# Keys with values in the second layer: five runs of small matmuls instead of eight

## The chip, the cores and the metric

The kernel runs on one core of a Trainium2 chip. The time is the device time of one execution, in microseconds (us), median of several runs. The engines are TensorE (PE: matmuls, and transposes as matmuls), VectorE (DVE), ScalarE (ACT), GpSimd (POOL) and SyncE (SP), which here issues the DMA transfers. Each engine works through its own queue of instructions in order, and waits on semaphores for what other engines must have finished.

## The reference

Four residual steps on x, 2048 rows of 640 columns: linear attention with learned features, a dense layer with mish, and the same two again with the same weights. What the change touches is the attention:

```python
qkv = (x @ wqkv).reshape(B, S, 3, H, Dh)            # H = 32 heads of Dh = 20
pk = jnp.einsum("bhsd,hdf->bhsf", k, w_phi)         # the same for q
phi_k = jnp.concatenate([softmax(pk), softmax(-pk)], axis=-1)
kv = jnp.einsum("bhsf,bhsd->bhfd", phi_k, v)
z = jnp.einsum("bhsf->bhf", phi_k)
o = einsum(phi_q, kv) / (einsum(phi_q, z) + 1e-6)
return o @ wo
```

`x` is layer-normalized ahead of it, and the result is added to x.

## The kernel before

**Tiles and stages.** The rows are cut into NB = 8 blocks of 256, a block into BT = 2 tiles of 128; tile i belongs to block i // 2. A layer's attention has two stages. The first (`attend_first`) goes through all blocks, projects them onto keys, queries and values, makes the features of keys and queries, and adds up features of keys times values over all rows in one PSUM tile, `kva`; the column of ones in each head's values makes z beside kv. The second (`attend_second`) turns `kva` into the weights `kvb` (L814), averages with them (L844), and projects with wo. The change concerns the first stage of the second layer (`layer` is 1); what comes ahead of it is the first layer's dense stage.

**A step.** A block has six steps, mostly in the order k0, k1, v0, v1, q0, q1 (keys, values and queries of its two tiles; the last block's q1 lies in stage 2, among its averages). Each step is a generator. `project` is 30 matmuls (L451): 5 slices of 128 columns, two halves, three products each, since a number is held as a high part (`xth`, weights `r1h`/`r2h`) and a low part (`xtl`, `r1l`/`r2l`). The low parts of the next block are made by POOL in three pieces, `lower` at L384: two of 128x512 for two slices each, and a third, 128x256, for the fifth slice. Within `project_half` the fifth slice's low part is first read by the 15th matmul.

**Features** (`features`, from L462). ACT evacuates the product (L135) into a `big` tile for keys, into `r210`/`r211` (the text of the profile has `r`) for queries; POOL has set their last columns to zero before (L467). DVE takes the largest and smallest of each head (L477), one engine subtracts the largest (L478: DVE for keys, POOL for queries), DVE the smallest (L480); ACT takes exp; DVE sums (L488) and inverts (L489); POOL multiplies by the inverse (L491, 128x1280). Queries are then transposed by DVE (L563, L561) and stored by SP in four transfers (L566) to `e_d`, from where stage 2 loads them (L783, L794, L796, L801) into `big` and `ol`.

**The sum.** When the features of keys are there, the generator `keys` goes on through some empty steps, `held(i)` of them, and then issues the tile's 32 matmuls of 40 columns into `kva` (L548; the profile counts 64 for a tile, 128 for two). `advance` moves all generators on by one step, the newest first, so `held` sets behind which step a tile's sum stands in PE's queue. In the second layer the two tiles of a block stand in one run behind the next block's first keys, the sum of block 1 behind block 2's second values, and the last block's at the end.

**Values** (`values`, `v_halves` at L142) are written by ACT into one tile of the pool `v` (2 buffers, one copy of 640 columns and one of the 32 ones), or into two smaller tiles of the pool `ol` (6 buffers, two copies of 320 and two of 16 ones), if `apart` is true. Features of keys lie in `big` (5 buffers).

**Order.** The order in which instructions enter the queues is that of a scheduler, which takes the program's order, its waits and `issue_after` into account. A shift on one engine therefore moves the order on others.

## Time and profile before

| what | value |
|---|---|
| median of three runs | 1348.87 us (1348.83 to 1349.65) |
| the profiled execution | 1349.24 us, of it the span 1347.4 |
| PE busy in 770 to 800 us | 30.00 of 30 us |
| DVE, ACT, POOL busy in 770 to 800 us | 25.69, 12.27, 17.16 us |
| granted clock of PE | 1.00 in all stretches looked at |

The times in all rows are microseconds from the start of the span. A row of the timeline has start, duration, engine, line, operation, output and inputs, shapes and a count; in brackets stands how long the engine was idle before, and what it waited for. Several instructions of one kind in a row are one line, with their common duration. A row of the chain of waits has start, duration, engine, line and count. The first stage of the second layer runs from about 694 us to 902 us.

### The profile page before, as it was taken

The numbers are of one execution on the slowest core, as the hardware profiler recorded it, in microseconds if no ns is written. First come the engines' busy times: TensorE is split into PE (matmuls) and PEld (weight loads), VectorE is DVE, ScalarE is ACT, GpSimd is POOL, SyncE is SP. The second block draws the span as 40 slices with busy tenths as digits, with TensorE's granted clock in tenths as the row PEclk, the third lists the DMA queues.
The fourth block names the chain that finished last, engine by engine and source line by source line (L and its number), as shares of the span: only waits on it lengthen the run. The fifth ranks groups of instructions, "written<-read, shape, count | busy, mean of one in ns | idle before, by whom it ended". The sixth has DMA issues, their size and how long they took to land.

```text
span 1347.4 us, 31386 instructions
## 1 busy us (share of the span) xinstructions
PE 1342.2 (100%) x13056; PEld 1333.4 (99%) x13056; DVE 1045.7 (78%) x1741; ACT 577.3 (43%) x986; POOL 480.2 (36%) x479
## 2 busy tenths in 40 slices
PE   9999999999999999999999999999999999999999
PEld 9999999999999999999999999999999999999998
DVE  6998898976787877778769788789759776676775
ACT  5444453223445545455443334332236444444443
POOL 3366554334322222222225556634352111111112
PEclk9999999999999999999999999999999999999999
DMA  9634446698703443234564534548873331233300
GB/s 329 195 91 91 95 87 148 167 268 304 221 18 87 118 118 81 56 100 114 152 213 111 130 80 96 94 111 265 262 270 107 79 91 23 84 98 99 79 21 21
DMA packets 353359, 174.24 MB, mean 129 GB/s; under 512 B 288193, under 2 KB 324785, under 8 KB 353217
## 3 DMA queue, kind: packets, MB, share of 16 engines
q1 hardware_dynamic: 353217, 172.25, 47.1%
q8 instruction: 102, 1.67, 0.5%
q14 instruction: 40, 0.33, 0.1%
HBM read 106.34 MB, written 65.86 MB: 128 GB/s over the span
## 4 chain that ended last, share of the span: by engine, by line
PE 100%; issue 0%; ACT 0%; DVE 0%; POOL 0%; POOLq 0%
PE mm L451 28%; PE one L969 25%; PE mm L1020 24%; PE one L451 13%; PE mm L844 3%; PE one L367 2%; PE one L548 2%; PE one L1020 1%; PE one L844 1%; PE one L92 0%; PE mm L274 0%; PE one L274 0%; PE mm L318 0%; ACT r1h L135 0%; PE one L811 0%
## 5 line engine op out<-in xcount | busy, mean ns | idle before, releaser
L995 POOL TENSOR_TENSOR ol<-big,ol 128x512 fp32r<-128x512 f32 (+1 forms) x98 | 131.9, 1346 | 471.7 <-ACT ol L994 411.6
L1020 PE MATMUL mm<-r2h,ol 128*128 128x320 f32 x1240 | 295.8, 309 | 0.0
L969 PE MATMUL one<-xtl,r1h 128*128 128x256 f32 x960 | 268.4, 280 | 0.0
L969 PE MATMUL one<-xth,r1l 128*128 128x256 f32 x960 | 268.2, 279 | 0.0
L969 PE MATMUL one<-xth,r1h 128*128 128x256 f32 x960 | 266.1, 280 | 0.0
L1020 PEld LDWEIGHTS mm<-r2h,ol 128*128 128x128 f32 x1240 | 212.1, 188 | 0.0
L1020 PE MATMUL mm<-r2l,ol 128*128 128x320 f32 x620 | 190.9, 309 | 0.0
L451 PE MATMUL mm<-r1h,xth 128*128 128x304 f32 (+1 forms) x600 | 184.6, 308 | 0.4 <-DVE r1l L334 0.4
L451 PE MATMUL mm<-r1l,xth 128*128 128x304 f32 (+1 forms) x600 | 183.7, 306 | 0.0
L451 PE MATMUL mm<-r1h,xtl 128*128 128x304 f32 (+1 forms) x600 | 183.5, 306 | 0.0
L969 PEld LDWEIGHTS one<-xth,r1l 128*128 128x128 f32 x960 | 180.5, 188 | 0.0
L969 PEld LDWEIGHTS one<-xtl,r1h 128*128 128x128 f32 x960 | 180.4, 188 | 0.0
L969 PEld LDWEIGHTS one<-xth,r1h 128*128 128x128 f32 x960 | 179.8, 188 | 0.0
L984 DVE TENSOR_SCALAR big<-big 128x512 f32<-128x512 f32 (+1 forms) x98 | 55.6, 567 | 120.8 <-ACT big L982 116.3
L982 ACT ACTIVATE big<-one,b1s 128x256 f32<-128x256 f32 x192 | 80.8, 468 | 102.4 <-PE one L969 102.1
L994 ACT ACTIVATE ol<-big 128x512 fp32r<-128x512 f32 (+1 forms) x98 | 60.8, 620 | 136.5 <-DVE big L993 136.4
L491 POOL TENSOR_TENSOR r<-r,r 128x1280 f32<-128x1280 f32 x32 | 79.0, 2468 | 110.6 <-DVE r L489 94.5
L1020 PEld LDWEIGHTS mm<-r2l,ol 128*128 128x128 f32 x620 | 116.5, 188 | 0.0
L986 ACT ACTIVATE big<-big,two 128x512 f32<-128x512 f32 (+1 forms) x98 | 70.1, 715 | 105.6 <-DVE big L985 105.5
L451 PEld LDWEIGHTS mm<-r1h,xth 128*128 128x128 f32 x600 | 112.8, 188 | 0.9 <-ACT r1h L135 0.5
L451 PEld LDWEIGHTS mm<-r1l,xth 128*128 128x128 f32 x600 | 112.8, 188 | 0.1
L451 PEld LDWEIGHTS mm<-r1h,xtl 128*128 128x128 f32 x600 | 112.8, 188 | 0.0
(179 smaller groups left out, 3132.9 us busy)
## 6 DMA issues: line engine op xcount, KB each, us to landing
e_d<-r SPq DMA_DIRECT2D x128, 160.0 KB, 4.0
big<-e_d SPq DMA_DIRECT2D x30, 640.0 KB, 8.9
x_d<-xt SPq DMA_DIRECT2D x23, 640.0 KB, 6.2
xt<-x_d SPq DMA_DIRECT2D x22, 640.0 KB, 5.3
n_d<-xn SPq DMA_DIRECT2D x168, 80.0 KB, 2.2
xt<-in_x SPq DMA_DIRECT2D x16, 640.0 KB, 4.6
xn<-x_d SPq DMA_DIRECT2D x28, 320.0 KB, 4.8
v<-n_d SPq DMA_DIRECT2D x30, 256.0 KB, 3.1
```

The costliest lines, as they stand in the source:

```text
L367: nc.tensor.transpose(ps[:, c, t * P:(t + 1) * P], self.rows[t][:, (c0 + c) * P:(c0 + c + 1) * P], ident)
L451: last_product[0] = nc.tensor.matmul(ps[:, :w], a[:, sl], r, start=(k == 0 and n == 0), stop=(k == KD - 1 and n == 2)).ins
L491: ins = scale.tensor_tensor(eg, eg, r.unsqueeze(2).to_broadcast([P, 2 * H, DH]), op=ALU.mult).ins
L548: nc.tensor.matmul(kva[32 * j:32 * j + DH + 1, 40 * r:40 * r + 40], v[1][c][:, (DH + 1) * g:(DH + 1) * (g + 1)], e[:, 40 * h:40 * h + 40], ...
L844: nc.tensor.matmul(po[c][64 * q:64 * q + 64, GW * j:GW * j + w], phs[g][:n, s0:s0 + 64], kvb[:n, g, :w], start=True, stop=True)
L969: nc.tensor.matmul(ph[:, j, :], l, r, start=(n == 0), stop=(n == 3 * KD - 1))
L982: exps[0] = nc.scalar.activation(part(ta, 0)[:, j - js.start], ph[:, j, :], AF.Exp, bias=b1s[:, 2 * pr + j:2 * pr + j + 1]).ins
L984: nc.vector.tensor_scalar_min(e, e, E_CAP)
L986: nc.scalar.activation(r, n, AF.Ln, bias=two)
L994: nc.scalar.activation(ah[:, js], n, AF.Copy)
L995: nc.gpsimd.tensor_tensor(al[:, js], n, ah[:, js].bitcast(F32), op=ALU.subtract)
L1020: ins = nc.tensor.matmul(pys[t][c][:, :HC], (ah, ah, al)[n][:, j, t * P:(t + 1) * P], w, start=(f == 0 and n == 0), stop=(f == KF - 1 and ...
```

## The change

`held` gets other numbers for the second layer, so that a sum of four tiles stands in one run: blocks 1 and 2 behind the first keys of block 3, blocks 3 and 4 behind the first keys of block 5, blocks 5 and 6 behind the first keys of block 7. Blocks 0 and 7 keep runs of two. As the values of two blocks then live at once, the second layer's blocks 4 and 6 put theirs in tiles of `ol`, as block 2 already did.

```diff
@@ -515,8 +515,8 @@
         def held(i):
 
             b, t = divmod(i, BT)
-            if layer and b == 1:
-                return 2
+            if layer and b in (1, 3, 5):
+                return 5 if b == 1 else 7 - t
             if not layer and b < 2:
                 return ((3, 1), (4, 1))[b][t]
             if not layer and b < NB - 2:
@@ -695,7 +695,7 @@
                 order = ("v0", "k0", "q0", "v1", "k1", "q1")
             elif b == NB - 1:
                 order = ("k0", "k1", "v0", "v1", "q0")
-            vs = [v_halves(b == 2 or (not layer and b % 2 == 0)) for _ in range(BT)]
+            vs = [v_halves(b % 2 == 0 and (b or not layer)) for _ in range(BT)]
             if 2 <= b < 2 + KD and not layer:
                 with tc.issue_after(last_act[0]):
                     o_ws.append(next(o_gen))
```

Three places in the queues, for the prediction. On PE, the sum of block 5 (`v` are its values, `r1h_...` the weights of the products around it, 64 matmuls a row) stood between the first and second keys of block 6:

```order
 L451 MATMUL mm<-r1l_8933,xth 128x304
 L451 MATMUL mm<-r1h_8932,xtl 128x304
-L548 MATMUL one<-big,v 21x40 x64
 L451 MATMUL mm<-r1h_8924,xth 128x304
 L451 MATMUL mm<-r1l_8925,xth 128x304
```

It is gone there; two blocks' sums now stand behind the first keys of block 7, those of block 6 (whose values are in `ol`) ahead of those of block 5:

```order
 L451 MATMUL mm<-r1l_8933,xth 128x304
 L451 MATMUL mm<-r1h_8932,xtl 128x304
+L548 MATMUL one<-big,ol 21x40 x64
 L548 MATMUL one<-big,v 21x40 x64
 L451 MATMUL mm<-r1h_8924,xth 128x304
```

The products themselves keep their order. On POOL, in block 3, where the low parts of block 4 are made (`xtl`, L384; `r_9941` and `r_9983` are the queries of block 2, `big` the keys of block 3), before:

```order
L491 TENSOR_TENSOR r_9941<-r_9941,r 128x1280
L384 TENSOR_TENSOR xtl<-xn,xth 128x512
L491 TENSOR_TENSOR r_9983<-r_9983,r 128x1280
L491 TENSOR_TENSOR big<-big,r 128x1280
L384 TENSOR_TENSOR xtl<-xn,xth 128x512
L467 MEMSET r_10281 128x32
L384 TENSOR_TENSOR xtl<-xn,xth 128x256
L491 TENSOR_TENSOR big<-big,r 128x1280
```

and now, where the queries of block 2 have other numbers:

```order
L491 TENSOR_TENSOR r_9877<-r_9877,r 128x1280
L491 TENSOR_TENSOR r_9919<-r_9919,r 128x1280
L384 TENSOR_TENSOR xtl<-xn,xth 128x512
L467 MEMSET r_10281 128x32
L491 TENSOR_TENSOR big<-big,r 128x1280
L384 TENSOR_TENSOR xtl<-xn,xth 128x512
L491 TENSOR_TENSOR big<-big,r 128x1280
L384 TENSOR_TENSOR xtl<-xn,xth 128x256
```

The first piece has moved behind the second query tile's L491, and the third behind the L491 of the second keys. On DVE, where stage 2 begins (`r_11637` is the first query tile of block 7, `kvb` the weights of the averages), before:

```order
L561 STREAM_TRANSPOSE r_11343<-r_11343 128x1280
L477 TENSOR_REDUCE m<-r_11637 128x32 x2
L814 TENSOR_TENSOR kvb<-one,mask 120x4x63 x2
L814 TENSOR_TENSOR kvb<-one,mask 120x3x63
L480 TENSOR_TENSOR r_11637<-m,r_11637 128x32x20
L853 TENSOR_SCALAR den<-mm 128x24
```

and now, the same tile under another number:

```order
L561 STREAM_TRANSPOSE r_11291<-r_11291 128x1280
L477 TENSOR_REDUCE m<-r_11649 128x32 x2
L480 TENSOR_TENSOR r_11649<-m,r_11649 128x32x20
L814 TENSOR_TENSOR kvb<-one,mask 120x4x63 x2
L814 TENSOR_TENSOR kvb<-one,mask 120x3x63
L853 TENSOR_SCALAR den<-mm 128x24
```

L480 has moved ahead of the three L814. In block 3, DVE's transposition of the first query tile (L563), too, stands earlier than before, ahead of the second keys' L477; and on SP the early loads of stage 2 into `ol` (L794, L796, L801) stand later.

## Prediction

> **What bounds the kernel now.** I read the page's busy shares first, then the list of TensorE's (PE's) waits, and then, for the stretch that the change touches, the chain of waits and the timelines of PE, POOL, DVE, ACT and SP.

> ```profile
> PE 1342.2 (100%) x13056; PEld 1333.4 (99%) x13056; DVE 1045.7 (78%) x1741; ACT 577.3 (43%) x986; POOL 480.2 (36%) x479
> ```

> ```profile
> PE one L92 <- POOL ident masks.py:199: 1.3, 1, 1.3
> PE mm L451 <- DVE r1l L334: 0.4, 1, 0.4
> PE one L274 <- issue: 0.2, 1, 0.2
> ```

> The whole span is matmul time: PE waits three times, 1.9 us in all, all at the start and none in the second layer. So the change can gain only what it takes out of PE's own stream, and it loses whatever wait it creates. The second layer's first stage in the chain of waits, one block of it, 27.2 us:

> ```profile
> 797.19 1.41 PE one L548 x126
> 798.60 25.78 PE mm L451 x180
> ```

> **What goes: three runs of small matmuls, not the matmuls.** A run of two tiles stands so on PE's timeline (start, duration of one or of the group):

> ```profile
> 796.75 0.30 PE L451 MATMUL mm<-r1l,xth 128*128 128x304 f32 x1
> 796.89 0.30 PE L451 MATMUL mm<-r1h,xtl 128*128 128x304 f32 x1
> 797.12 1.48 PE L548 MATMUL one<-big,v 128*21 128x40 f32 x128
> 798.52 0.41 PE L451 MATMUL mm<-r1h,xth 128*128 128x304 f32 x1
> 798.77 0.30 PE L451 MATMUL mm<-r1l,xth 128*128 128x304 f32 x1
> ```

> Projection matmuls start 0.14 us apart. From the last before the run (796.89) to the second behind it (798.77) it is 1.88, where two steps would take 0.28: the run costs 1.60. Its 128 matmuls span 1.48 less the last one's own duration, about 0.20 (an estimate: the profile gives the group only), so they are 10 ns apart, 1.28 together. The rest, 0.32 us, is paid once per run. The same number comes from the averages of stage 2, which already have a run of 88 and one of 176 matmuls:

> ```profile
> 902.13 0.30 PE L451 MATMUL one<-r2h,xtl 128*128 128x304 f32 x1
> ...
> 905.30 0.30 PE L451 MATMUL one<-r2l,xth 128*128 128x304 f32 x1
> ...
> 920.43 0.31 PE L451 MATMUL one<-r2h,xtl 128*128 128x320 f32 x1
> ...
> 926.18 0.31 PE L451 MATMUL one<-r2l,xth 128*128 128x320 f32 x1
> ```

> 88 take 3.17 - 0.28 = 2.89 and 176 take 5.75 - 0.29 = 5.46; two short runs less one long are 0.32. The 5-us run shows no slowing within. The change makes 8 runs into 5: **-0.95 us** (0.32 x 3), which I take as firm.

> **What is added on ACT.** Four value tiles are copied in halves.

> ```profile
> 751.42 0.77 ACT L135 ACTIVATE ol<-mm 128x320 f32<-128x320 f32 x2 [2.33 <-PE mm L451]
> 780.22 0.70 ACT L135 ACTIVATE v<-mm 128x640 f32<-128x640 f32 x1 [2.41 <-PE mm L451]
> ```

> Two halves take 0.07 us more than a whole, and a little again for the ones columns. ACT waits 2.3 to 2.4 us for PE ahead of these copies, and nothing on PE waits for them now: 0. Without that cover it would be 4 x 0.15 = 0.6.

> **What is moved on SP.** The `ol` tiles are held by values for longer, so stage 2's early loads into `ol` are issued later in SP's queue, and those queued behind them with them; the last wait for the run behind block 7's first keys, at about 879.

> ```profile
> 879.69 0.95 SPq L783 DMA_DIRECT2D big<-e_d x2
> 902.36 1.38 PE L844 MATMUL mm<-kvb,big 120*64 120x63 f32 x40
> ```

> ```profile
> big<-e_d SPq DMA_DIRECT2D x30, 640.0 KB, 8.9
> ```

> Before, the two loads of `big` stand at the same point, and their first reader, L844, starts 22 us later; from issue to landing such a load takes 8.9 us at the median. Six more in the same place share the queues, so I allow twice that, 18: 0, and up to 3 us if they took 25.

> **What is moved on POOL, third block.** The orders shown above put POOL's residual piece (L384) of the next block, first part, behind the second L491, and the third part behind one L491 on `big` more. Before:

> ```profile
> 782.68 1.29 POOL L384 TENSOR_TENSOR xtl<-xn,xth 128x512 fp32r<-128x512 f32 x1 [3.18 <-ACT xth L135]
> 785.26 2.37 POOL L491 TENSOR_TENSOR r<-r,r 128x1280 f32<-128x1280 f32 x1 [1.29 <-DVE r L489]
> 787.59 2.37 POOL L491 TENSOR_TENSOR big<-big,r 128x1280 f32<-128x1280 f32 x1
> 789.92 1.30 POOL L384 TENSOR_TENSOR xtl<-xn,xth 128x512 fp32r<-128x512 f32 x1
> 791.15 0.17 POOL L467 MEMSET r<- 128x32 f32 x1
> 791.23 0.75 POOL L384 TENSOR_TENSOR xtl<-xn,xth 128x256 fp32r<-128x256 f32 x1
> 791.93 2.38 POOL L491 TENSOR_TENSOR big<-big,r 128x1280 f32<-128x1280 f32 x1
> ```

> POOL works without a gap from 785.26. With the first L384 (1.3, until now in an idle stretch) and the second `big` (2.3) in that chain, the third part ends 3.6 later: 791.98 + 3.6 = 795.6. PE needs it in the 15th matmul of the next block's first keys. Those 30 matmuls end at the run at 797.1, so they start 30 x 0.14 earlier, at 792.8, and need it at 794.8; with one run switch gone already, 794.5. That is 1.1 late. DVE brings the second L491 its input earlier or later by some tenths, since it now transposes the first query tile ahead of the second keys, and both it and POOL follow a PE that is 0.3 ahead; by 0.8 earlier at best. Stall 0.3 to 1.1; I take **+0.7**, between.

> The lateness goes on into the fourth block, where the evacuation of its first queries (ACT `r<-mm`) must be done before PE can go on into the fifth block's keys:

> ```profile
> 789.56 0.68 ACT L135 ACTIVATE r<-mm 128x608 f32<-128x608 f32 x1 [2.55 <-DMA e_d<-r]
> 795.57 0.82 DVE L480 TENSOR_TENSOR r<-m,r 128x640 f32<-128x640 f32 x1 [2.67 <-POOL r L478]
> ```

> In the third block this copy ends at 790.2, 2.6 us ahead of the keys at 792.8. POOL and DVE enter the fourth up to 3.6 late less the 0.7 that PE itself stalls: 2.9 against 2.6. Bounds 0 (DVE's idle of 2.67 takes it up) and 0.5; **+0.2**. The blocks behind keep their order of residuals: 0.

> [...]

> ```profile
> 755.83 0.76 DVE L480 TENSOR_TENSOR big<-m,big 128x640 f32<-128x640 f32 x1
> 756.05 2.76 POOL L491 TENSOR_TENSOR r<-r,r 128x1280 f32<-128x1280 f32 x1 [0.81 <-DVE r L489]
> 778.30 1.88 DVE L478 TENSOR_TENSOR big<-big,m 128x640 f32<-128x640 f32 x1
> ```

> [...]

> **What is moved on DVE, start of stage 2.** L480 on block 7's first queries now stands ahead of the three L814, which make the weights of PE's first average.

> ```profile
> 899.84 1.50 DVE L477 TENSOR_REDUCE m<-r 128x32 f32<-128x640 f32 x2
> 901.63 1.01 DVE L814 TENSOR_TENSOR kvb<-one,mask 120x252 f32<-120x252 f32 x3 [0.29 <-PE one L811]
> 902.55 0.82 DVE L480 TENSOR_TENSOR r<-m,r 128x640 f32<-128x640 f32 x1
> ```

> ```profile
> 900.70 1.27 POOL L478 TENSOR_TENSOR r<-r,m 128x640 f32<-128x640 f32 x1 [1.86 <-DVE m L477]
> ```

> L480 waits for POOL's L478, which ends at 901.97; behind it stand L814, and behind L814 all of PE. So L480 runs to 902.8 and the first L814 (a third of 1.01) to 903.15. PE starts the average at 902.36 now, and so about as early with the terms above added up (-0.95 + 0.9): 0.8 late. DVE comes to L477 without a wait (its row names none), so it need not come forward when PE does; if it doesn't and PE has kept its 0.95, it is 1.75, and 2.2 with some tenths of lateness more. I take **+1.6**, nearer the upper end, since lateness adds.

> **Sum.** -0.95 + 0.7 + 0.2 + 1.6 = +1.55 us. The profiled execution took 1349.24 (span 1347.4), the median of the runs is 1348.87; on the median it makes **1350.4**.

> **Rivals.**
> 1. The stalls don't come: DVE and POOL find the idle time that their rows show (2.67 and 1.86 us of waits) and L480 is done in time. Then only the runs count, 1348.87 - 0.95 = **1347.9**. Against it: PE has no wait today, so nothing absorbs a late `kvb`.
> 2. Slower by more than 0.2%: DVE's two-operand steps fall under POOL's now gapless chain. Each such meeting costs DVE 1.06 (1.88 - 0.82), and a block that enters more than 2.6 us late passes it on. It decides if the fourth block ends later than it began: then the copies of queries are late for the sixth and seventh block too, by one meeting each: -0.95 + 0.7 + 0.2 + 2.1 + 2.2 = +4.25, **1353.1**. For it: the memsets and L491 stand in a new order in every block. Against it: in 80 us of blocks POOL has about 33 us idle and DVE 16:

> ```profile
> 800.00:880.00 80.00, 80.00 (x916) 79.34 (x914) 63.84 (x71) 30.62 (x45) 47.22 (x36) 1.00 0.42 80
> ```

> 3. The long runs slow down, since more weights are loaded in a row without a wide matmul to hide them: if the second half of each took half as long again, 0.64 a run, it is +1.9 on the sum, **1352.3**. Against it: the run of 176 above.
> 4. The loads are late for stage 2 by 3 us: -0.95 + 0.9 + 3 + 1.6, **1353.4**.
> That the runs don't merge at all is excluded by PE's order.

> **How the numbers follow.** The forecast has 0.50, rival 1 has 0.15, rival 2 0.23, rival 3 0.05, rival 4 0.04; 0.03 is left for a gain that I see no source for. 0.2% is 2.7 us, about what a measurement of this kernel can tell from no change. The forecast and rival 1 lie within it; rivals 2 and 4 outside, and half of 3. A tenth of the forecast (all its terms at their upper ends, +2.85) too. So faster 0.03, same 0.62, slower 0.35. Range: its low end is rival 1 with its own run-to-run spread, 1347.7; at the top it takes in rival 2 and a little of what may stall beyond it, to 1353.5. The likeliest case alone is 1349.1 to 1351.8.

> **What would show it.** Right: the chain has five L548 runs, three of about 2.9 us; PE's waits have new lines, L451 on POOL's `xtl` near 794 and L844 on DVE's `kvb` near 902, of some 0.7 and 1.6 us. Wrong: a wait of L451 on ACT or `r` in the fifth block or later over 0.5 us (rival 2), L844 on a DMA (rival 4), L548 of 256 longer than 3 us (rival 3), or no waits (rival 1). The sum itself is wrong if the three long runs save another amount than 0.3 each.

## Result and profile after

The change takes 1360.32 us (median of five runs, 1358.04 to 1361.01) against 1349.07 before (1348.83 to 1350.29): ratio 1.0078, interval 1.0067 to 1.0088, slower by 11.3 us. The prediction was 1350.4, within 1347.7 to 1353.5.

The page of the changed kernel, its row of busy times, and the list of PE's waits:

```profile
PE 1346.3 (99%) x13056; PEld 1338.0 (98%) x13056; DVE 1046.6 (77%) x1741; ACT 577.8 (43%) x994; POOL 481.3 (35%) x479
```

```profile
PE one L548 <- issue: 7.3, 3, 2.8
PE one L92 <- POOL ident masks.py:199: 1.3, 1, 1.3
PE mm L451 <- DVE r1l L334: 0.4, 1, 0.4
```

One line is new, and it is none of the waits that the prediction had named: PE stops three times in L548, 7.3 us in all, with no wait that the profile can name ("issue"). The list has no wait on `xtl`, `r` or `kvb`. The chain of waits shows where (start, duration, what):

```profile
768.14 2.12 PE one L548 x195
770.26 2.52 issue
772.78 0.76 PE one L548 x57
773.54 52.92 PE mm L451 x360
826.47 2.34 PE one L548 x217
828.81 1.98 issue
...
886.82 2.83 issue
```

Each long run is broken once. The products behind it take longer, too: 360 of them had 25.80 + 25.78 = 51.58 us before, now 52.92. The timeline of PE shows the break within the run, and the products behind it:

```profile
768.07 1.44 PE L548 MATMUL one<-big,ol 128*21 128x40 f32 x126
769.31 0.22 PE L548 MATMUL one<-big,v 128*21 128x40 f32 x2
769.33 0.21 PE L548 MATMUL one<-big,ol 128*21 128x40 f32 x2
769.35 0.90 PE L548 MATMUL one<-big,v 128*21 128x40 f32 x69
772.78 0.76 PE L548 MATMUL one<-big,v 128*21 128x40 f32 x57 [2.52 <-issue]
...
774.72 0.46 PE L451 MATMUL mm<-r1h,xth 128*128 128x304 f32 x1
774.98 0.46 PE L451 MATMUL mm<-r1l,xth 128*128 128x304 f32 x1
...
777.77 0.30 PE L451 MATMUL mm<-r1l,xth 128*128 128x304 f32 x1
777.91 0.30 PE L451 MATMUL mm<-r1h,xtl 128*128 128x304 f32 x1
```

Counted up, the stop comes behind the 199th matmul (126 + 2 + 2 + 69), in the midst of a tile whose first matmuls have been through: no matmul there has new data to wait for. In the second and third run it comes behind the 222nd and the 245th. Behind the stop the products are 0.25 us apart for three microseconds, and then 0.14 again. The table by stretches gives the granted clock there (it is the number ahead of the last two):

```profile
773.00:778.00 5.00, 5.00 (x76) 4.94 (x62) 3.02 (x4) 0.00 (x0) 1.99 (x2) 0.66 0.02 3
831.00:837.00 6.00, 6.00 (x63) 5.94 (x48) 2.26 (x3) 0.00 (x0) 2.52 (x2) 0.72 0.01 3
890.00:896.00 6.00, 6.00 (x32) 6.00 (x33) 2.74 (x4) 0.06 (x1) 2.37 (x1) 0.72 0.78 260
```

The lost clock is 0.34 x 5 + 0.28 x 6 + 0.28 x 6 = 5.1 us; within the first stretch, from 774.1 to 777.3, the clock is 0.50. A stop also costs more than its idle time: by PE's timeline, from the last product ahead of the first run (767.83) to the second behind it (773.72), less two steps, it is 5.61, where an unbroken run of 256 would take 2 x 1.60 - 0.32 = 2.88. That is 2.73 for a stop of 2.52, so 0.2 more. The profiled execution took 1361.01, 11.8 more than the one before: 7.3 + 3 x 0.2 for the stops, 5.1 for the clock, less 0.95 for the run switches, is 12.1, within 0.3 of it. The fastest run, 1358.04, had a mean clock of 0.998 where the profiled one had 0.996: 0.002 x 1359 = 2.7 us of their 3.0 (the clocks are rounded, so this can be off by 1).

**The theories.** A: PE's instructions run out. On the page, in the list of queues (packets, MB, share), before as after:

```profile
q8 instruction: 102, 1.67, 0.5%
```

PE executes 13056 matmuls and as many weight loads, 26112 instructions, and that is 102 x 256. So this queue seems to bring PE's program, in pages of 256 instructions or 128 matmuls (1.67 MB / 102 = 16.4 KB each); no row says what its packets hold. Kernels of the section below with another number of matmuls bear it out: 98 packets for 12544 matmuls (`e6_half` and `e7_half_before`; 98 x 256 = 2 x 12544), 103 for 13157 (`e3_fit`; 102.8 by that count). From the first stop to the second PE passes 57 + 360 + 222 = 639 matmuls, to the third 34 + 360 + 245 = 639: five pages less one matmul. The transfers of the queue also lie at the stops: one between 770.4 and 770.6, one between 828.2 and 828.4, one between 887.4 and 887.6. Each takes about 1 us, and PE goes on 1.3 to 1.4 us after its end (the first starts at 770.45, takes 0.93, and PE goes on at 772.78). B: a wait on late data of the older tiles that the profile doesn't see. C: what the change moved on POOL, DVE and SP. D: a limit of PE itself in a long stretch of small matmuls.

### The profile page after: what moved, and what is told of

Same layout as the page of the kernel before. It is cut to its first block, busy times and chain, and to the rows that moved or that the text cites. A ratio compares the mean times of both kernels' runs of the same rounds, so it can differ in the third digit from the quotient of the medians.

```text
span 1359.2 us, 31402 instructions
## 1 busy us (share of the span) xinstructions
PE 1346.3 (99%) x13056; PEld 1338.0 (98%) x13056; DVE 1046.6 (77%) x1741; ACT 577.8 (43%) x994; POOL 481.3 (35%) x479
## 3 DMA queue, kind: packets, MB, share of 16 engines
q8 instruction: 102, 1.67, 0.5%
## 4 chain that ended last, share of the span: by engine, by line
PE 98%; DMA 1%; issue 1%; ACT 0%; DVE 0%; SPq 0%
PE mm L451 28%; PE one L969 25%; PE mm L1020 24%; PE one L451 13%; PE mm L844 3%; PE one L367 2%; PE one L548 2%; PE one L1020 1%; PE one L844 1%; DMA raw<-in_wqk_t 0%; DMA big<-in_phi_bd 0%; PE mm L318 0%; PE mm L274 0%; PE one L274 0%; ACT r1h L135 0%
## 5 line engine op out<-in xcount | busy, mean ns | idle before, releaser
L451 PE MATMUL mm<-r1h,xth 128*128 128x304 f32 (+1 forms) x600 | 186.7, 311 | 0.4 <-DVE r1l L334 0.4
L451 PE MATMUL mm<-r1l,xth 128*128 128x304 f32 (+1 forms) x600 | 186.0, 310 | 0.0
L451 PE MATMUL mm<-r1h,xtl 128*128 128x304 f32 (+1 forms) x600 | 185.7, 309 | 0.0
L491 POOL TENSOR_TENSOR r<-r,r 128x1280 f32<-128x1280 f32 x32 | 80.1, 2503 | 109.7 <-DVE r L489 94.0
L451 PEld LDWEIGHTS mm<-r1h,xth 128*128 128x128 f32 x600 | 114.8, 191 | 0.8 <-ACT r1h L135 0.5
L451 PEld LDWEIGHTS mm<-r1l,xth 128*128 128x128 f32 x600 | 114.9, 191 | 0.1
L451 PEld LDWEIGHTS mm<-r1h,xtl 128*128 128x128 f32 x600 | 114.9, 191 | 0.0
```

What stands on the lines that cost most here:

```text
L451: last_product[0] = nc.tensor.matmul(ps[:, :w], a[:, sl], r, start=(k == 0 and n == 0), stop=(k == KD - 1 and n == 2)).ins
L491: ins = scale.tensor_tensor(eg, eg, r.unsqueeze(2).to_broadcast([P, 2 * H, DH]), op=ALU.mult).ins
```

## Experiments

**The sums apart, all other lines as in the change** (`e1_apart`).

```diff
-                return 5 if b == 1 else 7 - t
+                return 6 if b == 1 else 8 - t
```

> The older pair's sum stands one step later than in the change, behind 30 products: everything of the change stays (late sums, values in ol, the orders on POOL and DVE) but the four tiles are no longer one run. Theory A (PE's instructions run out in a run of 256 small matmuls): no wait of PE for 'issue', granted clock 1.00 throughout, eight runs; the 7.3 us of waits and the 5 us of low clock are gone, so 1349 to 1351, what is over 1349.1 being the stalls that the prediction named (0.7 at the low parts, 1.6 at kvb). Theory B (the late data of the older tiles makes PE wait): waits remain, now ahead of or within the later run, 1355 or more. Theory C (the move on POOL, DVE or SP costs the time): as in the change, 1360.

1354.65 us, ratio 1.0036 (1.0023 to 1.0050). The granted clock was 1.00 and no stop was left, as A has it. But it is 5.3 over before (1349.39, run again beside this and the next three; 1349.47 beside the last four), not up to 2. PE's waits in the second layer:

```profile
PE one L548 <- POOL big L491: 2.3, 1, 2.3
...
PE mm L451 <- POOL xtl L384: 1.3, 2, 0.8
PE mm L451 <- ACT r L135: 1.3, 1, 1.3
```

They are stalls of the kind that the prediction had looked for, 4.8 us of them: PE waits 0.48 for the low part at 795.6, 1.25 for the copy of the fourth block's queries at 820.8, 0.82 at 852.6 for a low part that is made in the fifth block, and 2.28 at 904.7 ahead of the last run of sums. In the change itself, whose PE is held up by the stops, none of them is in the list. Not all else is the same, though: POOL's order is nearly that of the change, but DVE's isn't. In the third block the change has the first query tile's L563 at 778.57, ahead of the second keys; here it stands behind their L478, at 780.82. So the 4.8 us need not be what the change would lose without its stops.

**40 matmuls ahead of the first long run** (`e2_shift`). Their results are not used; they share a tile with the sums and change these, here and in the next kernel.

```diff
+                if layer and n == 4 and b in {2: 40}:
+                    for _ in range({2: 40}[b]):
+                        nc.tensor.matmul(kva[:, 384:512], xts.hs[0][:, :P], q_ws[0][0][:, :P],
+                                         start=True, stop=True, skip_group_check=True)
```

> The change with 40 more matmuls of 128 columns (into unused columns of the sum's PSUM tile) in block 2, ahead of the first long run. Theory A: instructions come in pages of 256, which is 128 matmuls with their weight loads, so each of the three stops moves 40 matmuls ahead within its run: from behind matmul 199, 222 and 245 to behind 159, 182 and 205; lengths 2 to 2.8 us as before. Theory B (data) and theory D (a limit of PE in a long stretch of small matmuls): the stops stay at 199, 222 and 245.

1361.96 us in one execution. The timeline of the first long run:

```profile
772.58 1.44 PE L548 MATMUL one<-big,ol 128*21 128x40 f32 x126
773.82 0.22 PE L548 MATMUL one<-big,v 128*21 128x40 f32 x2
773.85 0.21 PE L548 MATMUL one<-big,ol 128*21 128x40 f32 x2
773.87 0.47 PE L548 MATMUL one<-big,v 128*21 128x40 f32 x29
776.57 1.19 PE L548 MATMUL one<-big,v 128*21 128x40 f32 x97 [2.23 <-issue]
```

126 + 2 + 2 + 29 = 159; in the other runs it is 182 and 205. All three stops have moved by the 40 matmuls, though nothing in the runs is changed. This speaks for A and against B and D: where PE stops goes with the count of its instructions from the program's start. The table by stretches gives that count (the x is the number of PE's matmuls); first the change, then this kernel, each up to its first stop:

```profile
0.00:770.26 770.26, 768.38 (x7620) 1.00 0.53 143
```

```profile
0.00:774.34 774.34, 772.18 (x7620) 1.00 0.53 142
```

The second and third stop come behind matmul 8259 and 8898, in both kernels. The DMA engines' load is not what the first stop here comes from: around it, from 774 to 777, their share is 0.00, and the stop is 2.23.

**The pages fitted to the runs** (`e3_fit`). As above, with `{2: 55, 4: 23, 6: 23}`.

> The change with 101 more matmuls of 128 columns, 55 ahead of the first long run, 23 more ahead of the second, 23 more ahead of the third, so that a page ends about 16 matmuls behind the start of each run and the next about 16 ahead of its end: most of each page's supply time then lies beside wide products. Theory A: the stops shrink to 0 to 0.6 us each and with them the low clock behind them; the 101 matmuls cost 0.06 to 0.1 us each, 6 to 10 us, so 1349.1 - 0.95 + 6 to 10 + 0 to 1.8 = 1354 to 1360, no slower than the change although it does more. Theories B and D: stops of 2 to 2.8 us as before, 1360.3 + 6 to 10 = 1366 to 1370.

1364.88 us (ratio 1.0116, 1.0103 to 1.0130): over the expectation, under that of B and D. PE's waits, and the first stop:

```profile
PE one L548 <- issue: 1.7, 3, 0.9
PE mm L451 <- issue: 1.6, 1, 1.6
```

```profile
776.22 0.33 PE L548 MATMUL one<-big,v 128*21 128x40 f32 x14
777.03 1.33 PE L548 MATMUL one<-big,v 128*21 128x40 f32 x112 [0.48 <-issue]
```

The stops come behind the 144th matmul, as reckoned, and are 0.48, 0.85 and 0.39 us; a fourth, 1.62, came in the products behind the third run, when the DMA engines were full (1.04 of their time between 895 and 898). The clock stayed at 1.00 in the stretches around all of them. Counted from the program's start they are 7620, 8259 and 8898 again, and 9026, 128 later. The time is 4.9 over the expected 1360. The 101 matmuls took 11.0 us (the first 55 of them 6.09, 0.111 each) instead of at most 10, and the stops 3.3 instead of at most 1.8. The saving of 0.95 doesn't show either: in the chain of waits the way from the first product of the stage to the first average is 14.7 longer than before, which is 11.0 + 3.3 and 0.3 more. The last 1.5 have no one place.

**The smaller value tiles alone** (`e5_values`): the second hunk of the change on the kernel before.

> The kernel before with the second part of the change alone: values of the second layer's blocks 4 and 6 in ol, the sums where they were. All theories but C: 1349.1, within 0.5. Theory C: if the smaller copies or the later loads into ol cost, 1351 or more.

1349.68 us, ratio 1.0005 (0.9996 to 1.0014). This part costs nothing that can be measured; PE's waits are those of before.

**Half as many instructions** (`e6_half`, on the change; `e7_half_before`, on the kernel before).

```diff
-            for r in range(9):
+            w = 80 if layer else 40
+            for r in range(4 if layer else 9):
...
-                        nc.tensor.matmul(kva[32 * j:32 * j + DH + 1, 40 * r:40 * r + 40],
-                                         v[1][c][:, (DH + 1) * g:(DH + 1) * (g + 1)], e[:, 40 * h:40 * h + 40],
+                        nc.tensor.matmul(kva[32 * j:32 * j + DH + 1, w * r:w * r + w],
+                                         v[1][c][:, (DH + 1) * g:(DH + 1) * (g + 1)], e[:, 40 * h:40 * h + w],
```

> The change, where each matmul of the second layer's sums takes 80 columns and only 16 of 32 heads are taken (half of the sums is left out): a tile's sum takes PE about as long as before, but in half as many instructions, so a run of four tiles has 128 matmuls. The orders on POOL and DVE are nearly those of the kernel before here. Theory A (instructions run out): no stop, full clock, and what was meant by the change appears: 0.9 less than e7_half_before. Theory D (PE can't sustain a long stretch of small matmuls): stops of 2 us or more in each run of four, 7 to 12 us more than e7_half_before.

> The kernel before with the same half sums of 80 columns, as the base for e6_half. If 80 columns take twice as long as 40, within 0.5 us of the kernel before; all theories agree on it.

1347.47 us, ratio 0.9990 (0.9980 to 1.0000), and 1350.55, ratio 1.0001 (0.9991 to 1.0011). A run of two and a run of four tiles in `e6_half`, with a product ahead and the second one behind:

```profile
720.42 0.31 PE L451 MATMUL mm<-r1h,xth 128*128 128x320 f32 x1
720.66 1.30 PE L549 MATMUL one<-big,v 128*21 128x80 f32 x64
...
722.15 0.31 PE L451 MATMUL mm<-r1h,xtl 128*128 128x320 f32 x1
...
767.83 0.30 PE L451 MATMUL mm<-r1h,xtl 128*128 128x304 f32 x1
768.06 1.30 PE L549 MATMUL one<-big,ol 128*21 128x80 f32 x64
769.18 1.29 PE L549 MATMUL one<-big,v 128*21 128x80 f32 x64
770.40 0.41 PE L451 MATMUL mm<-r1h,xth 128*128 128x304 f32 x1
770.64 0.30 PE L451 MATMUL mm<-r1l,xth 128*128 128x304 f32 x1
```

No stop in 2.3 us of small matmuls, where PE had run 2.1 to 2.6 before its stops in the change: with half the instructions, four tiles fit. A run of two costs 722.15 - 720.42 less 0.29 for two steps of a product, 1.44; a run of four 770.64 - 767.83 - 0.28 = 2.53. Two short ones less a long one are 0.35, where the prediction had 0.32. So the saving is there when no stop falls into the run. The difference of 3.1 between the two kernels isn't this alone: `e7_half_before` has 1.8 us of waits on DVE, POOL and ACT in its list, in an order of its own, and `e6_half` has none of them in this stage. The ten executions of `e7_half_before` lie in two groups, four from 1347.96 to 1348.75 and six from 1350.49 to 1352.15; the profile is of the slower group. Why there are two isn't shown.

**Twice the time for each instruction** (`e8_wide`): `w = 80` as above, with all nine `r`, the output columns left at `40 * r` and the input's start held at 1200 at most, so the sums overlap.

> The change, where each matmul of the second layer's sums takes 80 columns instead of 40 (all heads, overlapping sums): as many instructions, twice the time for each. Theory A: a page lasts 1.3 us longer within the run, so the stops stay behind about matmul 199 of the first run and shrink from 2 to 2.8 us to 0.5 to 1.5; time 1349.4 - 0.95 + 10.2 for the wider matmuls + 1.5 to 4.5 = 1360 to 1363. Theory D by count: stops as long as in the change, 1370.

1365.55 us in one execution. The rows behind the stops of the first and third long run, and in the chain of waits the stop of the second:

```profile
776.07 1.30 PE L550 MATMUL one<-big,v 128*21 128x80 f32 x57 [0.73 <-issue]
...
895.51 0.61 PE L550 MATMUL one<-big,v 128*21 128x80 f32 x20 [0.95 <-issue]
```

```profile
835.78 0.14 issue
```

The order has put 26 matmuls of the second run and 10 of the third 16 products ahead, but all three stops lie behind matmul 7620, 8259 and 8898 of the program, as in the change. They are 0.73 instead of 2.52, 0.14 instead of 1.98 and 0.95 instead of 2.83, although the second run now lasts 5 us. With D a longer stretch of small matmuls should stop longer. The time is over the expectation by 2.6, and PE's waits on ACT's copies (2.7 us, L451 on `r`) are that much.

**One long run of three** (`e4_one`).

```diff
-            if layer and b in (1, 3, 5):
-                return 5 if b == 1 else 7 - t
+            if layer and b in (1, 5):
+                return 2 if b == 1 else 7 - t
```

> Only blocks 5 and 6 are summed in one run, the others as before (the order puts 16 of the 256 matmuls 15 products ahead, so the run has 240); values as in the change. Theory A: one stop, behind about the 229th of the 240, 2 to 2.8 us, and the low clock behind it in some executions: 1351 to 1354. If the cost were that of the values in ol or of the late sums in general: nearer 1349.5.

1354.61 us, ratio 1.0035 (1.0023 to 1.0047): above the expected 1354, with

```profile
PE one L548 <- issue: 2.9, 1, 2.9
...
PE mm L844 <- DVE kvb L814: 0.7, 1, 0.7
```

One stop, behind the 220th matmul of the run of 240 (expected 229) and the 8898th of the program, as in the change, and behind it the wait on `kvb` that the prediction had described, since this kernel has L480 ahead of L814 as well. The clock of the profiled execution was 1.00 behind a stop of 2.9, so a stop alone doesn't settle whether the clock falls.

**How long a page takes.** The 14 stops of the change, `e2_shift`, `e3_fit`, `e8_wide` and `e4_one` have two things in common. They lie at the same counts of matmuls, which B, C and D would not give in five kernels. And in the traces' DMA records the last packet of the instruction queue ahead of PE's restart ends 1.3 to 1.6 us before it, in each (1.40, 1.26 and 1.30 in the change). So the stops go with that queue; that PE waits for a page of its program is read from the two together, as no row names what it waits for. When a page is asked for, no row shows either. An estimate: if that is 160 matmuls ahead of the page's first (a page and 32 matmuls; the 32 are fitted to these stops), the time from there to the end of the stop comes out as 4.4, 3.8 and 4.6 us in the change, and as 4.4, 4.8 and 4.3 in `e3_fit`, where 144 matmuls and 16 products lie in it. For the fourth stop there it is 6.3, with the DMA share at 1.04. In the kernel before, the 160 matmuls around a run of two have some 31 products among them (an estimate from the order: 31 x 0.14 + 129 x 0.010 + 0.3 for the switches, 5.9 us), and PE never stops.

## Why the prediction was wrong

- **"-0.95, which I take as firm"** failed, and with it the price of rival 3. The saving per merged run was sized rightly (0.35 in `e6_half` for 0.32). But the prediction held that a longer run costs only its matmuls. The 256 cost 2.0 to 2.8 us of stop each, 0.2 more for the break, and some 1.7 of low clock, where rival 3 had 0.64. What the sum left out are these stops, by theory A the supply of PE's own instructions.
- **Rival 3 came by its sign and not by its cause.** Its sign, an L548 run of 256 longer than 3 us, is there (5.4 for the first). But it had weights that load more slowly in the second half of a run, and the matmuls are 10 ns apart ahead of the stop and behind it (69 in 0.90 us and 57 in 0.76, less 0.2 for the last).
- **The evidence against rival 3 was misread.** The run of 176 in stage 2 has its matmuls 29 ns apart, so that a page of 128 lasts 3.7 us, and the 160 from the supposed request to the use 4.7. The runs in question have 10 ns, and a page lasts 1.28. That this is why the one doesn't stop is argued from the times above, not tested by itself. What counted was not the run's length in us (the second run of `e8_wide` lasts 5 us and stops for 0.14), but instructions in a given time, and the row that could have told it, 102 packets of the instruction queue, wasn't read.
- **Rival 2, 1.06 for a meeting**: the kernel before has the figures. DVE's L478 on 128x640 took 0.82 at the median of 32, and 1.88 at 778.30, where POOL's L491 ran from 777.13 to 779.50. In no run is the cost of one such meeting measured by itself.
- **ACT and SP at nothing**: right, by `e5_values` (1.0005).
- **The low part, +0.7, in the third block**: 0.48 in `e1_apart`, within its bounds, in another order of DVE. In the change POOL ends the third piece at 795.43 (the prediction had 795.6), but PE comes to its first product on it at 798.47, held up by the first stop and the low clock: 3.0 to spare. **The fourth block, +0.2**: 1.25 in `e1_apart`, over the bound of 0.5; DVE's idle time did not take up the lateness. In the change that copy ends at 819.44, and PE needs it at 822.11. A low part made in the fifth block, put at 0, cost 0.82.
- **Start of stage 2, +1.6**: in `e1_apart` the wait came one step earlier, 2.28 on POOL's L491 on the last keys; in `e4_one` it was the wait on `kvb` that was named, 0.7, just under the lower bound of 0.8. Its chain was right in kind.
- These stalls make 4.8 us in `e1_apart` where the sum had 2.5, but in the change none of them is in PE's list. For the two stalls above the times show why: DVE, POOL and ACT are about as far as in `e1_apart` or ahead, and PE comes 2.7 to 3.0 us after them. For the others it is the likely reason.
- **The bounds of the likeliest case** add up to 1349.0 and 1351.7 (-0.95 + 0.3 + 0.8 and -0.95 + 1.1 + 0.5 + 2.2 on 1348.87), 0.1 below those stated; nothing hangs on it.
- **The bound on a gain** (nothing beyond 0.95, since PE waits nowhere) stands. What the prediction missed is that a PE without waits can also lose to stops that no data of the program sets, 7.3 us here.

No version with runs of four came out faster with the whole of the sums. At the position that was fitted to the pages, `e3_fit`, a run still loses 0.4 to 0.9 us, more than the 0.32 that it saves.

## What to carry to other kernels

Before small matmuls are put together, count PE's instructions per time. Here runs of 240 and 256 matmuls, 10 ns apart, stopped PE for 1.9 to 2.9 us each (the change, `e2_shift`, `e4_one`), and runs of 128 (the kernel before) did not. In this kernel 128 matmuls with their weight loads are a page, and by the estimate above, which rests on the fitted 160, one needs some 4 to 5 us to come; by it the 160 matmuls ahead of a page must last that long. Fewer and wider matmuls (`e6_half`) and shorter runs (`e1_apart`) had no stop; with the runs shifted against the pages (`e3_fit`) each still lost 0.4 to 0.9 us. A wait with the releaser "issue" in the midst of such a run, at a fixed count from the program's start (7620, 8259 and 8898 here), is the sign; shift the program by some instructions and see whether it moves. A stall predicted for a late engine can be real and yet not show, when something larger delays the engine that would wait.
